# Softmax scaling: one operation for each head of a pair over all four pairs, in place of one operation for each pair of heads

## The chip, the cores and the metric

The kernel runs on one core of one Trainium2 chip. The metric is the device time of one execution in microseconds (us), of which less is better. Besides the time there is a profile of one execution: every instruction of each engine with its start and duration. The engines are called PE (TensorE; PEld is its weight load), DVE (VectorE), ACT (ScalarE), POOL (GpSimd) and SP (SyncE, which here only issues DMAs).

## What is computed

Two layers follow each other. The first is a dynamic convolution: each position of a sequence has, for each of 8 heads, 7 weights that a softmax makes; the output of a head at position s is the weighted sum of its 24 channels at positions s-6 to s. The second is a feed-forward layer with a squared ReLU.

```python
# x: (8, 4096, 192), weight_gen: (8, 4096, 8, 7), all float32
w = weight_gen - np.max(weight_gen, axis=-1, keepdims=True)
w = np.exp(w)
w = w / (np.sum(w, axis=-1, keepdims=True) + 1e-09)
...
out = np.einsum('bshk,bskhg->bshg', w, x_unf)     # x_unf: 7 positions back, per head of 24 channels
...
h = np.maximum(x @ w_in, 0.0)                     # 192 -> 2048
return (h * h @ w_out).astype(np.float32)         # 2048 -> 192
```

## The kernel before

The 32768 positions are cut into 64 sub-blocks of 512 and these into 33 blocks: two of one sub-block, then 31 of two. The instructions of all engines follow an order written out by hand: for each block a string of steps ("plan", L666 to L674, run by the loop at L782), in which a letter stands for a stage.

- L, E, S: the softmax of a part of a sequence. `load` (L213) fetches the raw weights. E is `exp` (L238) on ACT, float32, written as `ex` with the order row, pair g, tap k, head of the pair e. S is `soft` (L747): `total` (L256, a DVE reduction over the taps), `recip` (L263, a DVE reciprocal into `rcp`) and `scale` (L266, the changed function). A partition holds R consecutive positions (32 for most parts, 16 or 8 for the first ones) and 6 more of the next partition, so that 38, 22 or 14 rows are scaled. They come in pieces (`CUTS`, L682), for R = 32 of 8, 10, 10 and 10 rows, one piece per block of the main loop (`TIMES`, L685, and the default at L709).
- `scale` multiplies `ex` by the broadcast `rcp` and writes float16 into `v`, a tile [row, pair g, slot of 8, head e] (`v_big`, or `v_first` for parts of 8 rows per partition). The row stride is 64 elements, but tap k of a row lands one row further on and the slot moves with the row, which is what the strides H*SL and H*SL + 2 in the output's pattern do. Since the slots wrap every 8 rows, `scale` cuts its rows at multiples of 8 (L270): a piece of 8 rows is one cut, rows 18 to 28 are 6 and 4.
- The result goes to DRAM (`store`, L284, on SP's queue) and back as `wr` (`wr_load`, L349, SP), or, for the parts of 8 rows, straight from SBUF to SBUF (`wr_load_sbuf`, L354, DMAs at L363 on SP and POOL).
- B: `st_band` (L371, L381) multiplies `wr` by a mask on DVE into `bd`, the banded matrix of the convolution.
- C: `st_conv` (L466) or, from block 8 on, `st_conv_spread` (L429): PE multiplies `xt` by `bd` (L487, L450), then ACT and DVE copy the sum to `y` (L503, L460).
- u: `st_unit` (L508): PE makes 128 hidden features of a block, or 256 in the two small ones (L518), ACT applies the ReLU (`t`, L532, from 3 buffers that hold two units each), DVE squares (`g`, L536), two units at once up to unit 13 of a block from block 4 on.
- M: half of a quarter of the second product (`st_mm2`, L548, PE at L560) for the block before; it reads 8 of the 16 `g` of its block as weights. After the second half ACT and DVE sum and SP stores (L574, L576, L581).

DVE, ACT and POOL each execute in the order of the program. On DVE a piece of softmax thus stands between the copies, squares and bands of its block.

Of the kernel before, what the change touches and what calls it, by code (L numbers as in the profile page):

```python
# [9 lines left out]
def kernel(  # L10
# [31 lines left out]
    H, KK = weight_gen.shape[2], weight_gen.shape[3]  # L42
# [7 lines left out]
    HP = H // 2  # L50

    P = 128
# [9 lines left out]
    SL = 8  # L62
# [139 lines left out]
    class Softmax:  # L202
# [63 lines left out]
        def scale(self, lo, hi, eng):  # L266

            v = self.v
            while lo < hi:
                n = min(SL - lo % SL, hi - lo)  # L270
                for g in range(HP):
                    eng.tensor_tensor(  # L272
                        out=bass.AP(
                            tensor=v.tensor,
                            offset=v.offset + lo * H * SL + lo % SL * 2 + g * SL * 2,
                            ap=[list(v.ap[0]), [H * SL + 2, n], [H * SL, KK], [1, 2]],
                        ),
                        in0=self.ex[:, lo : lo + n, g],
                        in1=self.rcp[:, lo : lo + n, g].unsqueeze(2).broadcast_to((P, n, KK, 2)),
                        op=AluOp.mult,  # L280
                    )
                lo += n
# [312 lines left out]
    with nc.allow_low_precision("fp16 matmul pipeline"), tc.manual_schedule():  # L595
# [3 lines left out]
        for b in range(B):  # L599
            t0 = 0  # L600
            for r in PARTS.get(b, (R,)):
                v = v_first[len(parts) % 2] if r == FIRST else v_big
# [97 lines left out]
        for n, s in enumerate(parts):  # L700
            k = n - min(m for m, p in enumerate(parts) if p.b == s.b)
# [4 lines left out]
        for n, s in enumerate(parts[4:], 4):  # L706
            b, f = s.b, s.fb
            k = n - min(m for m, p in enumerate(parts) if p.b == b)
# [73 lines left out]
        for j in range(NBLK):  # L782
# [3 lines left out]
            for step in plans[j].split():  # L786
                kind, n = step[0], int(step[1:] or 0)
# [73 lines left out]
```

The softmax here doesn't subtract the row's maximum and nothing guards it: scores larger than these inputs give would overflow.

## Time and profile before

| | |
|---|---|
| time, median of 3 runs | 734.74 us (734.73 to 734.76) |
| profiled execution: its own time | 734.93 us |
| profiled execution: span from first to last instruction | 733.2 us |
| PE busy | 726.3 us, 99% of the span |
| DVE busy | 627.3 us, 86%, 856 instructions |
| ACT busy | 613.8 us, 84% |
| the changed operation, L272 on DVE | 228 instructions, in 38 groups of 4 or 8 |
| granted PE clock | 1.0 throughout |

How to read it: the busy time of an engine says how much of the span it was executing something. PE's share overstates its load, since the ends of matmuls are modelled. A timeline line gives the start in us, the duration, the engine, the line of the kernel, the operation with its output and input tile, how many such instructions are merged into the line, and in brackets how long the engine had been idle before it and what ended that. Times in groups are sums over the whole run.

### The profile page before, as it was taken

The page shows a single profiled execution, that of the slowest core. Times are in us where ns is not written, and L with a number is a line of the kernel's source. Part 1 is how long each engine was busy: PE and PEld are TensorE (multiplying, and loading weights), DVE is VectorE, ACT ScalarE, POOL GpSimd, SP SyncE. Part 2 cuts the span into 40 slices and gives each one's busy share as a digit, 9 for nine tenths or more (in the row PEclk, how much of TensorE's full clock was granted, in tenths as well). Part 3 has the DMA queues.
Part 4 walks back from the last instruction along what each step waited for, and adds up shares of the span by engine and source line. Part 5 has one row for each costly group of instructions (what it writes and reads, how often), then busy time and mean ns, then how long its engine had stood idle before and what let it go on. Part 6 is the DMA issues. An engine that isn't in the chain of part 4 may idle for free.

```text
span 733.2 us, 31124 instructions
## 1 busy us (share of the span) xinstructions
PE 726.3 (99%) x14106; PEld 528.5 (72%) x14106; DVE 627.3 (86%) x856; ACT 613.8 (84%) x724; POOL 100.5 (14%) x148
## 2 busy tenths in 40 slices
PE   8999999999999999999999999999999999999998
PEld 4767777777777777777777777777777777777777
DVE  5999898998898988888988888988889988778753
ACT  5998888988888888888888888888888888888883
POOL 7322222320001100011000010010100110001000
PEclk9999999999999999999999999999999999999999
DMA  7745444794445442455433464334544315444012
GB/s 216 124 88 132 81 63 106 143 164 119 93 73 117 105 86 64 71 131 112 69 70 72 115 125 82 62 68 122 104 87 85 59 49 120 66 87 78 30 45 67
DMA packets 126544, 68.71 MB, mean 94 GB/s; under 512 B 85193, under 2 KB 122636, under 8 KB 125900
## 3 DMA queue, kind: packets, MB, share of 16 engines
q1 hardware_dynamic: 80908, 48.12, 23.0%
q0 software_dynamic: 45360, 18.50, 21.6%
q8 instruction: 110, 1.80, 1.0%
q14 instruction: 22, 0.18, 0.1%
q10 hardware_dynamic: 144, 0.10, 0.0%
HBM read 50.18 MB, written 28.70 MB: 108 GB/s over the span
## 4 chain that ended last, share of the span: by engine, by line
PE 96%; DVE 1%; DMA 1%; ACT 1%; issue 0%; DVEq 0%
PE o L560 47%; PE h L518 45%; PE yp L450 4%; PE yp L487 1%; DVE bd L381 1%; DMA wr<-v_first 1%; ACT t L532 0%; DMA wg<-in_weight_gen_dram 0%; ACT ex L250 0%; DVE v_first L272 0%; ACT y L503 0%; DVE ssum L257 0%; DVE rcp L264 0%; DVE g L536 0%; DVE xt L347 0%
## 5 line engine op out<-in xcount | busy, mean ns | idle before, releaser
L532 ACT ACTIVATE t<-h 128x1024 f16<-128x1024 f32 x512 | 496.5, 1026 | 59.9 <-PE h L518 59.5
L560 PEld LDWEIGHTS <-g 64*128 64x128 f16 (+1 forms) x8032 | 342.5, 94 | 55.9 <-issue 2.5
L560 PE MATMUL o<-w_o,g 64*128 64x192 f16 (+1 forms) x8032 | 379.0, 243 | 0.0
L536 DVE TENSOR_TENSOR g<-t 128x2048 f16<-128x2048 f16 (+1 forms) x309 | 309.3, 1037 | 28.1 <-ACT t L532 27.9
L518 PE MATMUL h<-y,w_p 64*128 64x512 f16 x2400 | 291.7, 376 | 0.0
L518 PEld LDWEIGHTS <-w_p 64*128 64x128 f16 x2400 | 113.8, 94 | 94.9
L381 DVE TENSOR_TENSOR bd<-wr,mask 128x4160 f16<-128x4160 f16 (+3 forms) x89 | 149.4, 1703 | 4.1 <-DMA wr<-v_first 4.1
L576 DVE TENSOR_TENSOR o_sb<-o,o_sb 128x384 f32<-128x384 f32 x123 | 68.4, 556 | 60.8 <-ACT o_sb L574 59.8
L333 POOL DMA_DIRECT2D xt<-in_x_dram x62 | 52.1, 843 | 421.6 <-PE yp L450 362.5
L574 ACT COPY o_sb<-o 128x384 f32<-128x384 f32 x129 | 61.6, 478 | 46.7 <-PE o L560 45.9
L518 PE MATMUL h<-y,w_i 64*128 64x512 f16 (+1 forms) x768 | 82.1, 350 | 1.8 <-ACT t L532 0.8
L518 PEld LDWEIGHTS <-w_i 64*128 64x128 f16 x768 | 36.1, 94 | 28.6 <-issue 4.0
L450 PEld LDWEIGHTS <-xt 128*32 128x32 f16 x2000 | 24.5, 95 | 10.6 <-issue 10.6
L272 DVE TENSOR_TENSOR v_big<-ex,rcp 128x112 f16<-128x112 f32 (+5 forms) x180 | 29.8, 236 | 1.8 <-DMA vd<-v_big 0.8
L460 DVE CAST y<-yp 128x1024 f16<-128x1024 f32 x25 | 30.4, 1218 | 0.0
L450 PE MATMUL yp<-bd,xt 128*32 128x104 f16 (+1 forms) x2000 | 28.3, 210 | 0.0
L250 ACT ACTIVATE ex<-wg 128x560 f32<-128x560 f32 (+4 forms) x38 | 25.9, 682 | 1.7 <-DMA wg<-in_weight_gen_dram 1.7
L257 DVE TENSOR_REDUCE ssum<-ex 128x80 f32<-128x560 f32 (+4 forms) x38 | 25.3, 666 | 2.2 <-ACT ex L250 2.2
L460 ACT CAST y<-yp 128x1024 f16<-128x1024 f32 x25 | 25.2, 1006 | 0.0
L264 DVE RECIPROCAL rcp<-ssum 128x80 f32<-128x80 f32 (+4 forms) x38 | 22.8, 600 | 1.3
L323 POOL DMA_DIRECT2D xt<-in_x_dram x7 | 3.9, 553 | 124.7 <-PE yp L450 109.7
L363 POOL DMA_DIRECT2D wr<-v_first x31 | 16.9, 563 | 16.0 <-DVE v_first L272 15.8
(34 smaller groups left out, 97.3 us busy)
## 6 DMA issues: line engine op xcount, KB each, us to landing
out_dram<-o_sb SPq DMA_DIRECT2D x63, 384.0 KB
xt<-in_x_dram POOLq DMA_DIRECT2D x42, 240.0 KB, 5.0
wg<-in_weight_gen_dram SPq DMA_DIRECT2D x4, 1064.0 KB
xt<-in_x_dram POOLq DMA_DIRECT2D x20, 192.0 KB, 4.7
wr<-vd SPq DMA_DIRECT2D x38, 80.0 KB
vd<-v_big SPq DMA_DIRECT2D x5, 512.0 KB
y<-y SPq DMA_DIRECT2D x100, 24.0 KB
wg<-in_weight_gen_dram SPq DMA_DIRECT2D x5, 392.0 KB
```

What stands on the lines that cost most here:

```text
L250: nc.scalar.activation(out=self.ex[:, lo:hi].rearrange("p r g k e -> p (r g) k e"), in_=self.wg[:, lo:hi].rearrange("p r (g e) k -> p (r g ...
L272: eng.tensor_tensor(out=bass.AP(tensor=v.tensor, offset=v.offset + lo * H * SL + lo % SL * 2 + g * SL * 2, ap=[list(v.ap[0]), [H * SL + 2, ...
L333: eng.dma_start(out=dst[:, first:last], in_=ap)
L381: nc.vector.tensor_tensor(out=bd_t[j][:, H * lo : H * (lo + len(tiles) * n)].rearrange("p (g m c) -> p g m c", g=shape[1], c=2 * SL), in0= ...
L450: nc.tensor.matmul(out=yp[p0 : p0 + 32, k - k0, a:b], lhsT=x_t[s][:, i, c0 : c0 + 32], rhs=bd[:, head // 2, e, 0 : b - a], start=True, sto ...
L460: copy(out=y[:, k0 : k0 + 2], in_=yp)
L518: nc.tensor.matmul(out=h[:, half, jj * th : (jj + 1) * th], lhsT=w_in_chunk(w, u * per + jj, slot, half), rhs=y_t[j][r0 : r0 + RT, k, 0:th ...
L532: nc.scalar.activation(out=t1[:, e], in_=h, func=ActF.Relu)
L536: nc.vector.tensor_tensor(out=g[:, a : e + 1], in0=t1[:, a : e + 1], in1=t1[:, a : e + 1], op=AluOp.mult)
L560: nc.tensor.matmul(out=oo[:, cc * Dm : (cc + 1) * Dm], lhsT=g[r0 : r0 + n, cc * P : (cc + 1) * P], rhs=w_o[r0 : r0 + n, fc, :], start=(fc ...
L574: nc.scalar.copy(out=o_sb, in_=o[0][:, c])
L576: nc.vector.tensor_tensor(out=o_sb, in0=o[1][:, c], in1=o_sb, op=AluOp.add)
```

## The change

In `scale` the loop over the four pairs of heads becomes a loop over the two heads of a pair. Nothing else differs but the line numbers after it, which are 3 higher.

```diff
                 n = min(SL - lo % SL, hi - lo)
-                for g in range(HP):
+                for e in (0, 1):
                     eng.tensor_tensor(
                         out=bass.AP(
                             tensor=v.tensor,
-                            offset=v.offset + lo * H * SL + lo % SL * 2 + g * SL * 2,
-                            ap=[list(v.ap[0]), [H * SL + 2, n], [H * SL, KK], [1, 2]],
+                            offset=v.offset + lo * H * SL + lo % SL * 2 + e,
+                            ap=[list(v.ap[0]), [H * SL + 2, n], [SL * 2, HP], [H * SL, KK]],
                         ),
-                        in0=self.ex[:, lo : lo + n, g],
-                        in1=self.rcp[:, lo : lo + n, g].unsqueeze(2).broadcast_to((P, n, KK, 2)),
+                        in0=self.ex[:, lo : lo + n, :, :, e].rearrange("p r g k -> p (r g) k"),
+                        in1=self.rcp[:, lo : lo + n, :, e]
+                        .rearrange("p r g -> p (r g)")
+                        .unsqueeze(2)
+                        .broadcast_to((P, n * HP, KK)),
                         op=AluOp.mult,
                     )
```

A cut of n rows took four operations of 14n elements per partition and takes two of 28n. Before, the innermost loop ran over the two heads of a pair: two neighbours in `ex` (float32), two neighbours in `rcp`, two neighbours in `v` (float16, 4 bytes together), then a hop of 128 bytes in `v` to the next tap. After, the innermost loop runs over the seven taps of one head: every second element of `ex` (8 bytes apart), the same element of `rcp` seven times, and in `v` single elements of 2 bytes that lie 128 bytes apart.

## The prediction

> **What bounds the kernel now.** I read the page first (busy times, chain of waits), then the groups by form, then two stretches of the timeline: the start and one block of the steady part.
>
> ```profile
> PE 726.3 (99%) x14106; PEld 528.5 (72%) x14106; DVE 627.3 (86%) x856; ACT 613.8 (84%) x724; POOL 100.5 (14%) x148
> ...
> PE 96%; DVE 1%; DMA 1%; ACT 1%; issue 0%; DVEq 0%
> PE o L560 47%; PE h L518 45%; PE yp L450 4%; PE yp L487 1%; DVE bd L381 1%; DMA wr<-v_first 1%; ACT t L532 0%; DMA wg<-in_weight_gen_dram 0%; ACT ex L250 0%; DVE v_first L272 0%; ACT y L503 0%; DVE ssum L257 0%; DVE rcp L264 0%; DVE g L536 0%; DVE xt L347 0%
> ```
>
> The chain that ended last is PE for 96%. DVE is on it for 1%, and the changed line only at the start. So a shorter scaling can win next to nothing; a longer one costs only where DVE becomes so late that PE waits. The groups by form give the price of the operation now, by its width:
>
> ```profile
> L272 DVE TENSOR_TENSOR v_big<-ex,rcp 128x112 f16<-128x112 f32 x60 | 12.5, 271 | 1.4 <-DMA vd<-v_big 0.8
> L272 DVE TENSOR_TENSOR v_big<-ex,rcp 128x84 f16<-128x84 f32 x52 | 9.3, 241 | 0.2
> L272 DVE TENSOR_TENSOR v_big<-ex,rcp 128x56 f16<-128x56 f32 x32 | 4.8, 211 | 0.1
> L272 DVE TENSOR_TENSOR v_big<-ex,rcp 128x28 f16<-128x28 f32 x20 | 2.4, 181 | 0.0
> ```
>
> From 28 to 112 elements it grows by 90 ns, 1.07 ns an element over 151 ns fixed. The timeline shows four of 112 in 0.83 us, so they start (0.83 - 0.271) / 3 = 0.186 us apart: 85 ns of each overlap the next, and a group takes 85 ns + 66 ns for each operation + 1.07 ns for each element.
>
> The timeline of a steady block (start, duration, engine, line):
>
> ```profile
> 406.42 1.22 DVE L272 TENSOR_TENSOR v_big<-ex,rcp 128x84 f16<-128x84 f32 x8
> ...
> 407.56 2.35 DVE L536 TENSOR_TENSOR g<-t 128x2048 f16<-128x2048 f16 x2
> ...
> 409.83 0.55 DVE L576 TENSOR_TENSOR o_sb<-o,o_sb 128x384 f32<-128x384 f32 x1
> ...
> 410.93 2.52 DVE L536 TENSOR_TENSOR g<-t 128x2048 f16<-128x2048 f16 x3 [0.55 <-ACT t L532]
> ...
> 412.71 1.47 PEld L560 LDWEIGHTS <-g 64*128 64x128 f16 x32
> 412.93 1.48 PE L560 MATMUL o<-w_o,g 64*128 64x192 f16 x32
> ```
>
> After the scaling DVE stands idle once, for 0.55 us, then squares the last three units of the block until 413.45. PE's next M starts at 412.93; its last eighth, which needs the last square, starts 7/8 of some 1.31 us later, at 414.08. So that M has 0.63 us in hand; less 0.22 us by which the weight load goes ahead and some 0.06 us of signalling, 0.35 us. DVE may come 0.55 + 0.35 = 0.9 us late from this scaling before PE waits. The other steady blocks repeat this (0.38 us idle after the few groups of 1.28 us).
>
> **What the Trainium skill says.** (1) "Vector Engine (DVE) Microarchitecture Reference", 5.2 Measured stream behaviour: two-source operations take 1.0417 ns a column plus about 75 ns an instruction after overlap. The trace agrees: 1.07 and 66. (2) The same section, on the SBUF access granule: a port streams at full rate only if consecutive elements come in runs of at least two adjacent 4-byte words; a destination that hops at every element takes 1.71 ns a column (4 KiB hops) or 2.50 (hops of 24 words), all three ports hopping 1.98. The trace has no such write; today's, two halves of one word and then a hop, runs at full rate. (3) "SBUF — State Buffer", Door 1, on 16-byte cachelines: full rate needs two hits on a line. The trace's L257, which reads every second float32 of `ex`, agrees: 448 elements in 610 ns and 560 in 726, 1.04 ns each.
>
> **The change, part by part.**
>
> Removed and added: 228 operations become 114 of twice the width. Over all widths they carry 60x112 + 24x112 + (52+24)x84 + 32x56 + 20x28 + 8x70 + 8x42 = 19,040 elements, the same as before. Fewer instructions save 114 x 66 ns = 7.5 us of DVE. Against that stands s, the time per element. Full rate, 1.07 ns, is the low end: then DVE saves 7.5 us. The write now hops 128 bytes at every element, the first source steps by two words, the second repeats a word. Page prices: 1.71 to 2.50 for such a destination alone; if the sources add to it as in the page's three-port row (1.98 / 1.71 = 1.16), up to 2.9. I take 2.3, an estimate inside these prices, as 32 words lie nearer to the row with 24 than to the one with 4 KiB. Then DVE gets 19,040 x 1.23 = 23.4 us more and 7.5 less: +16 us. It breaks even at s = 1.07 + 7.5/19.04 = 1.46.
>
> Steady groups (560 elements, 8 operations now, 4 then): 85 + 4x66 + 560 s. At 1.07: 0.95 us (before: 1.22); at 2.3: 1.64, +0.42; at 2.9: 1.97, +0.75. All are below the 0.9 us in hand: hidden by DVE's idle time and M's reserve. Without this cover it would cost 0.42 us in each of some 17 blocks, 7 us. The price that uses up the cover is (1.22 + 0.9 - 0.349) / 0.56 = 3.2 ns an element. The reserve of the `t` buffers at unit 14 is larger (1.8 us or more in these blocks).
>
> Behind the scaling on SP's queue stand the store to DRAM and the `wr` loads; bands need those half a block (some 11 us) later, so +0.4 us is hidden. POOL's DMAs of `wr` are issued when the scaling ends and move with it; none is added.
>
> The start (784 elements, 8 operations to 4) is on the chain:
>
> ```profile
> 6.70 1.46 DVE L272 TENSOR_TENSOR v_first<-ex,rcp 128x112 f16<-128x112 f32 x8
> ...
> 8.19 1.93 SPq L363 DMA_DIRECT2D wr<-v_first  x3
> ...
> 11.98 1.47 ACT L650 CAST w_i<-w_st 128x1536 f16<-128x1536 f32 x1 [0.15 <-DMA w_st<-in_moe_w_in_dram]
> 12.27 2.60 DVE L381 TENSOR_TENSOR bd<-wr,mask 128x832 f16<-128x832 f16 x5 [4.11 <-DMA wr<-v_first]
> ```
>
> It becomes 0.35 + 0.784 s: 1.19 us at 1.07 (-0.27), 2.15 at 2.3 (+0.69), 2.62 at 2.9 (+1.16). But the first `wr` lands 4.1 us after its issue, where the median of these DMAs is 2.6: it stands in SP's DMA queue behind the weights `w_st`, whose last landing ends a wait at 11.98. So up to some 1.4 us later issue is hidden, and an earlier one gains little. I take 0.
>
> Early blocks with less cover. (a) The second part (22.88 to 24.34) delays the bands that end at 33.17; PE's convolution starts at 33.87. Reserve 0.7; +0.69 just fits: some 0.1. (b) Around 98 to 104 DVE is full: two groups of 448 elements (86.11 and 101.68, each +0.42 at 2.3) with 0.2 us idle between them, ahead of an M with 0.78 - 0.28 = 0.5 us in hand: 0.84 - 0.2 - 0.5 = 0.1. (c) The other early groups of 448 have 0.5 us or more of idle or reserve ahead: 0. Sum +0.2 us. At 2.5 it is some 0.5, at 2.9 some 1.3 (0.5 at each of (a) and (b), 0.3 elsewhere).
>
> The sum against the profiled execution: 734.93 + 0.2 = 735.1; that stands 0.19 above the median, so 734.74 + 0.2 = 734.9.
>
> **The rivals.**
>
> (A) Forecast: hopping writes at 1.7 to 2.9 ns, hidden. 734.7 to 736.0, likeliest 734.9. For it: PE's 96% and DVE's idle time; against it: how close the reserves are to what is added.
>
> (B) Full rate: short 4-byte hops are free as L257's reads are, or the write port merges them. DVE saves 7.5 us of busy time, PE doesn't care; the start gains 0.27 us at most, half of it behind `w_st`: 734.6. Speaks for it that today's writes hop every 2 elements without cost.
>
> (C) Slower: 2-byte writes that share no word cost over 3.2 ns, for instance because a partial word has to be read first (nothing here shows that). It happens at M after each block's last square: at 4 ns a group takes 2.59 us, +1.37, of which 0.47 passes 0.9 us and stops PE, in some 17 blocks 8 us, with the early ones 10: 745. At 3.3 it is 737. It decides from 3.2 ns. Against it: the largest page price is 2.5.
>
> (D) Faster by over 0.2%: DVE is full from 18 to 43 us and relief there would have to reach PE. The groups there save 0.27 + 0.13 + 0.1 us: too little.
>
> That the change doesn't do what it says: built, it has 114 operations of 128 x (n x 4 x 7) in the same places; excluded.
>
> **How the numbers follow.** 0.2%, 1.5 us, is about what a measurement of this kernel can tell from no change. A 0.60, of which 0.06 above 1.5 us; B 0.14; C 0.22, of which 0.20 above; D 0.04. So faster 0.04, same 0.70, slower 0.26. The likeliest time is 734.9. Leaving out D and the part of C beyond 3.4 ns (about 0.15) gives 734.3 to 738.0.
>
> **What would show it.** L272 has 114 instructions; one of 224 elements takes 151 + 224 s: 0.39 us at full rate, 0.67 at 2.3, 0.87 at the limit of 3.2. DVE busy rises by some 16 us. The idle time before the third-last square of a block shrinks from 0.55 to some 0.1, and the wait list shows no PE wait for `g`. The first bands still start near 12.3. I am wrong if an instruction of 224 takes over 0.87 us, if the first bands move with the scaling, or if the M after a block's end starts late, block after block.

## The result and the profile after

The changed kernel takes 767.23 us (median of 6 runs, 765.56 to 767.91) against 734.74: 1.0442 times, with a 95% interval of 1.0429 to 1.0456, so 32.5 us more. The prediction said 734.9, with a range up to 738.0. The profiled execution took 765.56 us with a span of 763.9, 30.7 more than the span before.

The page of the changed kernel, its busy times and its chain:

```profile
PE 733.5 (96%) x14106; PEld 567.0 (74%) x14106; DVE 671.3 (88%) x742; ACT 614.1 (80%) x724; POOL 99.9 (13%) x148
...
PE 67%; DVE 24%; DMA 3%; issue 3%; ACT 2%; POOL 1%; DVEq 0%; POOLq 0%; SPq 0%
PE o L563 36%; PE h L521 28%; DVE g L539 6%; DVE v_big L272 6%; PE yp L453 3%; DVE o_sb L579 3%; DVE v_first L272 3%; DVE rcp L264 2%; DVE ssum L257 2%; DMA wr<-v_first 2%; DVE bd L384 1%; ACT o_sb L577 1%; DMA vd<-v_big 1%; POOL wr L366 1%; ACT t L535 0%
```

DVE executes 114 instructions fewer and is busy 44 us longer. It was on the chain for 1% and now is for 24%. Its groups by form say why (last columns: busy time, mean ns of one):

```profile
L272 DVE TENSOR_TENSOR v_big<-ex,rcp 128x224 f16<-128x224 f32 x30 | 32.7, 1283 | 4.2 <-DMA vd<-v_big 3.6
L272 DVE TENSOR_TENSOR v_big<-ex,rcp 128x168 f16<-128x168 f32 x26 | 23.1, 1083 | 0.2
...
L272 DVE TENSOR_TENSOR v_big<-ex,rcp 128x112 f16<-128x112 f32 x16 | 10.3, 838 | 0.1
...
L272 DVE TENSOR_TENSOR v_big<-ex,rcp 128x56 f16<-128x56 f32 x10 | 4.4, 638 | 0.0
```

From 56 to 224 elements the operation grows by 645 ns: 3.84 ns an element, where it was 1.07. An operation of 112 elements, a form that both kernels have, took 271 ns and takes 838. Now the wait lists. PE's longest wait of the changed kernel is not in the list of the kernel before at all (us in total, times, longest):

```profile
PE o L563 <- DVE o_sb L579: 19.6, 24, 3.6
```

The timeline of the changed kernel shows why, in the block just before the one that the prediction showed (both scale 10 rows, and before the change both run alike):

```profile
407.24 2.68 DVE L272 TENSOR_TENSOR v_big<-ex,rcp 128x224 f16<-128x224 f32 x4
...
409.54 2.55 DVE L539 TENSOR_TENSOR g<-t 128x2048 f16<-128x2048 f16 x2
...
411.78 0.24 PE L563 MATMUL o<-w_o,g 64*128 64x192 f16 x1
412.01 0.55 DVE L579 TENSOR_TENSOR o_sb<-o,o_sb 128x384 f32<-128x384 f32 x1
412.48 2.41 DVE L539 TENSOR_TENSOR g<-t 128x2048 f16<-128x2048 f16 x3
412.61 1.48 PE L563 MATMUL o<-w_o,g 64*128 64x192 f16 x31 [0.59 <-DVE o_sb L579]
```

PE starts an M at 411.78 and comes through one matmul. The product is summed in two banks of PSUM, the memory that PE writes to: ACT copies the first (L577), DVE adds the second (L579), and the next M may write the second bank only when this add has read it. The add stands on DVE behind the scaling and two squares. It ends at 412.56, and 0.05 us later PE goes on. The same scaling, add and M before:

```profile
384.33 1.22 DVE L272 TENSOR_TENSOR v_big<-ex,rcp 128x112 f16<-128x112 f32 x8
...
387.74 0.55 DVE L576 TENSOR_TENSOR o_sb<-o,o_sb 128x384 f32<-128x384 f32 x1
...
388.87 1.48 PE L560 MATMUL o<-w_o,g 64*128 64x192 f16 x32
```

The add ended at 388.29, so it had 0.58 us in hand. From the start of the scaling to the end of the add it was 3.96 us and is 5.32, 1.36 more; the block (from one scaling to the next, 384.33 to 406.42 before, 407.24 to 430.16 now) takes 22.92 us instead of 22.09, 0.83 more. 1.36 - 0.83 = 0.53: what was in hand, but for the signalling.

The trace can be read block by block, if the start of the second matmul of each M is compared in the two traces. (A block counts here with the M of its own units, which runs in the block after it.) The delay is 4.2 us by the end of block 1, 9.3 by the end of block 4, 13.1 after block 5 (which adds 3.8), 16.8 after block 8, and 30.7 after block 27, the last with a scaling. In the steady part, from block 12 on, each block with a piece of 10 rows adds 0.83, each with a piece of 8 rows only 0.1: there the shorter sum, reciprocal and scaling leave the add some 0.6 us more. Blocks 9 to 11, whose pieces are cut otherwise, add 0.9 to 1.3 each.

### The profile page after: what moved, and what is told of

Its sections match the earlier page's. It is cut to its first block, busy times and chain, and to the rows that moved or that the text cites. A ratio compares the mean times of both kernels' runs of the same rounds, so it can differ in the third digit from the quotient of the medians.

```text
span 763.9 us, 31010 instructions
## 1 busy us (share of the span) xinstructions
PE 733.5 (96%) x14106; PEld 567.0 (74%) x14106; DVE 671.3 (88%) x742; ACT 614.1 (80%) x724; POOL 99.9 (13%) x148
## 4 chain that ended last, share of the span: by engine, by line
PE 67%; DVE 24%; DMA 3%; issue 3%; ACT 2%; POOL 1%; DVEq 0%; POOLq 0%; SPq 0%
PE o L563 36%; PE h L521 28%; DVE g L539 6%; DVE v_big L272 6%; PE yp L453 3%; DVE o_sb L579 3%; DVE v_first L272 3%; DVE rcp L264 2%; DVE ssum L257 2%; DMA wr<-v_first 2%; DVE bd L384 1%; ACT o_sb L577 1%; DMA vd<-v_big 1%; POOL wr L366 1%; ACT t L535 0%
## 5 line engine op out<-in xcount | busy, mean ns | idle before, releaser
L563 PE MATMUL o<-w_o,g 64*128 64x192 f16 (+1 forms) x8032 | 391.9, 243 | 20.5 <-DVE o_sb L579 19.6
L563 PEld LDWEIGHTS <-g 64*128 64x128 f16 (+1 forms) x8032 | 354.2, 94 | 71.5 <-issue 31.8
L539 DVE TENSOR_TENSOR g<-t 128x2048 f16<-128x2048 f16 (+1 forms) x309 | 314.0, 1060 | 13.3 <-ACT t L535 13.2
L521 PE MATMUL h<-y,w_p 64*128 64x512 f16 x2400 | 298.0, 376 | 0.0
L521 PEld LDWEIGHTS <-w_p 64*128 64x128 f16 x2400 | 141.4, 94 | 73.5
L579 DVE TENSOR_TENSOR o_sb<-o,o_sb 128x384 f32<-128x384 f32 x123 | 69.2, 563 | 60.8 <-ACT o_sb L577 60.2
L577 ACT COPY o_sb<-o 128x384 f32<-128x384 f32 x129 | 61.6, 478 | 44.4 <-PE o L563 42.2
L521 PE MATMUL h<-y,w_i 64*128 64x512 f16 (+1 forms) x768 | 83.8, 350 | 2.5 <-ACT t L535 1.3
L272 DVE TENSOR_TENSOR v_big<-ex,rcp 128x224 f16<-128x224 f32 (+5 forms) x90 | 69.1, 1035 | 4.6 <-DMA vd<-v_big 3.6
L521 PEld LDWEIGHTS <-w_i 64*128 64x128 f16 x768 | 42.7, 94 | 24.6 <-issue 5.5
L272 DVE TENSOR_TENSOR v_first<-ex,rcp 128x224 f16<-128x224 f32 (+1 forms) x24 | 22.9, 1179 | 0.3
```

The costliest lines, as they stand in the source:

```text
L272: eng.tensor_tensor(out=bass.AP(tensor=v.tensor, offset=v.offset + lo * H * SL + lo % SL * 2 + e, ap=[list(v.ap[0]), [H * SL + 2, n], [SL ...
L521: nc.tensor.matmul(out=h[:, half, jj * th : (jj + 1) * th], lhsT=w_in_chunk(w, u * per + jj, slot, half), rhs=y_t[j][r0 : r0 + RT, k, 0:th ...
L539: nc.vector.tensor_tensor(out=g[:, a : e + 1], in0=t1[:, a : e + 1], in1=t1[:, a : e + 1], op=AluOp.mult)
L563: nc.tensor.matmul(out=oo[:, cc * Dm : (cc + 1) * Dm], lhsT=g[r0 : r0 + n, cc * P : (cc + 1) * P], rhs=w_o[r0 : r0 + n, fc, :], start=(fc ...
L577: nc.scalar.copy(out=o_sb, in_=o[0][:, c])
L579: nc.vector.tensor_tensor(out=o_sb, in0=o[1][:, c], in1=o_sb, op=AluOp.add)
```

## The experiments

**What makes the operation dear.** Six kernels change L272 alone. The first two split writes from reads. In the first, with the writes of the changed kernel, the edit is

```diff
-                        in0=self.ex[:, lo : lo + n, :, :, e].rearrange("p r g k -> p (r g) k"),
-                        in1=self.rcp[:, lo : lo + n, :, e]...
+                        in0=self.ex[:, lo : lo + n, 2 * e : 2 * e + 2].rearrange("p r g k c -> p r (g k c)"),
+                        in1=self.ex[:, lo : lo + n, 2 - 2 * e : 4 - 2 * e].rearrange("p r g k c -> p r (g k c)"),
```

> Writes as in the changed kernel (single float16 elements 128 bytes apart), both sources read in order instead (two different quarters of the exponentials, so the weights are wrong). Theory W, the write alone makes the price: an operation of 224 elements stays at 1.29 us and the time near 766 us. Rival S, the strided and repeated sources make it: 0.39 us and the time near 735 us. Both together: in between, some 0.7 us.

The second keeps the sources and writes to neighbours:

```diff
-                            offset=v.offset + lo * H * SL + lo % SL * 2 + e,
-                            ap=[list(v.ap[0]), [H * SL + 2, n], [SL * 2, HP], [H * SL, KK]],
+                            offset=v.offset + lo * H * SL + e * H * SL // 2,
+                            ap=[list(v.ap[0]), [H * SL, n], [KK, HP], [1, KK]],
```

> Sources as in the changed kernel (every second exponential, the reciprocal seven times), written to neighbouring float16 elements (so the weights lie in wrong places). Theory W: an operation of 224 elements takes some 0.39 us, since the sources run at full rate, and the time goes back to 734 to 735 us. Rival S: 1.29 us and near 766 us.

The groups by form, first with the write alone changed as in the changed kernel, then with the reads alone:

```profile
L272 DVE TENSOR_TENSOR v_big<-ex 128x224 f16<-128x224 f32 x30 | 31.7, 1248 | 3.6 <-DMA vd<-v_big 3.6
```

```profile
L272 DVE TENSOR_TENSOR v_big<-ex,rcp 128x224 f16<-128x224 f32 x30 | 10.4, 388 | 1.3 <-DMA vd<-v_big 0.7
```

1248 of the 1283 ns come with the write; with the changed reads and a dense write the rate is still 1.07 ns an element. The times, one execution each: 760.8 us and 734.2, beside 734.1 for the kernel before. Theory W holds, though the first time is 5 us under the 766 expected: in its trace a steady block loses 0.65 us, not 0.83. The second kernel also shows what a cheaper scaling is worth: DVE is busy 620.9 us, 6.4 less than before, and the time is the same within 0.2 us.

The other four change the write further: whole words of float32 at the same 128 bytes (by a comparison in place of the product), and half words (single float16 elements, half of a 4-byte word) at 4, 8 and 16 bytes. The edits in short, each to the output's pattern:

```diff
+ whole words:  v32 = v viewed as float32; [H * SL // 2 + 1, n], [SL, HP], [H * SL // 2, KK]; op=AluOp.is_ge
+ 4 bytes:      offset + e; [H * SL, n], [KK * 2, HP], [2, KK]
+ 8 bytes:      offset + e; [2 * H * SL, n], [4 * KK, HP], [4, KK]
+ 16 bytes:     offset + e; [H * SL, n], [2, HP], [8, KK]
```

> As the changed kernel, but each write is a whole float32 word, 128 bytes from the last (the operation is a comparison, whose result is 0 or 1, instead of the product; both heads write the same words, so the weights are wrong). If the hop of 128 bytes makes the price: 1.29 us for 224 elements. If it is the half word: at most the 1.7 to 2.5 ns that the skill gives for hopping words, so 0.5 to 0.75 us.

> As the changed kernel, but the float16 elements are written 4 bytes apart instead of 128 (so the weights lie in wrong places): still half a word each, but four on a line of 16 bytes. If the half word makes the price: 1.29 us for 224 elements. If it is the hop to another line: near 0.39 us.

> As the changed kernel, but the float16 elements are written 16 bytes apart (so the weights lie in wrong places): every element on another line of 16 bytes. If a half word on another line is what costs: 1.29 us for 224 elements and some 766 us. If it takes a long hop: near 0.41 us and 735 us.

> As the changed kernel, but the float16 elements are written 8 bytes apart (so the weights lie in wrong places): two elements on a line of 16 bytes. If two on a line are enough, as the skill says of lines: near 0.41 us for 224 elements. If the unit is 8 bytes: 1.29 us.

The groups of the four, in the order words, 4, 16 and 8 bytes:

```profile
L273 DVE TENSOR_TENSOR v_big<-ex,rcp 128x224 f32<-128x224 f32 x30 | 17.2, 572 | 3.3 <-DMA vd<-v_big 2.2
```

```profile
L272 DVE TENSOR_TENSOR v_big<-ex,rcp 128x224 f16<-128x224 f32 x30 | 10.7, 409 | 1.4 <-DMA vd<-v_big 0.8
```

```profile
L272 DVE TENSOR_TENSOR v_big<-ex,rcp 128x224 f16<-128x224 f32 x30 | 32.4, 1268 | 4.0 <-DMA vd<-v_big 3.4
```

```profile
L272 DVE TENSOR_TENSOR v_big<-ex,rcp 128x224 f16<-128x224 f32 x30 | 17.5, 683 | 2.2 <-DMA vd<-v_big 1.7
```

With the operations of 56 elements from the same lists (264, 218, 639 and 307 ns) the slopes are:

| write, one element after the other | ns an element | 128x224, ns | time of the kernel, us |
|---|---|---|---|
| float16 neighbours (reads as changed) | 1.07 | 388 | 734.2 |
| float16, 4 bytes apart | 1.14 | 409 | 735.0 |
| float32 word, 128 bytes apart | 1.83 | 572 | 736.0 |
| float16, 8 bytes apart | 2.24 | 683 | 735.2 |
| float16, 16 bytes apart | 3.74 | 1268 | 767.4 |
| float16, 128 bytes apart (the change) | 3.84 | 1283 | 767.2 |

The last row is a median of six executions, the others are one each; the kernel before took 734.1 us beside the 4-byte, dense and whole-word cases, and 735.0 (median of nine) beside those of 8 and 16 bytes. Neither the half word alone (4 bytes apart: 1.14) nor the hop alone (a whole word: 1.83) makes this price. Half words that each lie on another 16 bytes make it, and 128 bytes cost hardly more than 16. Why that is so, no run shows. The 8 byte case came out between the two answers expected: two elements on a line of 16 bytes are not enough for the full rate of such writes, otherwise than the prediction's third point has it for lines. Each kernel up to 2.24 ns stays within 2 us of the kernel before: the loss starts somewhere between 2.24 and 3.74.

**Is it DVE's lateness that PE pays for, or something else in the scattered writes?** The kernel before, with each scaling operation done twice:

```diff
-                for g in range(HP):
+                for g in (*range(HP), *range(HP)):
```

> The kernel before with every scaling operation done twice, so DVE is kept as late by cheap writes: a group of 560 elements takes 85 + 16 x 66 + 1120 x 1.07 ns = 2.34 us, 1.12 more than before (the changed kernel: 1.47 more). Theory Q, a late DVE delays the add that frees the PSUM bank of the second product, with 0.63 us in hand for 560 elements and 1.24 for 448: each 560 block loses some 0.5 us, the early part 4 to 6, together 745 to 750 us. Rival I, the scattered writes disturb the other engines at SBUF: 735 us.

It took 753.46 us, 1.0246 times the kernel before (1.0230 to 1.0263): rival I falls for the steady part, for these writes are the old ones. A steady block lost 0.60 with a group 1.13 us longer, so again 0.53 us was in hand, and blocks with 8 rows lost nothing. The total is 3 us above the range expected; the early blocks lost 10.7, not 4 to 6. Its wait list has the same entry:

```profile
PE o L560 <- DVE o_sb L576: 11.4, 22, 2.7
```

**Which wait.** The changed kernel, with the add taken off the PSUM bank, its place and length kept:

```diff
-            nc.vector.tensor_tensor(out=o_sb, in0=o[1][:, c], in1=o_sb, op=AluOp.add)
+            nc.vector.tensor_tensor(out=o_sb, in0=o_sb, in1=o_sb, op=AluOp.add)
```

> The changed kernel, but the DVE add of the output reads the SBUF tile twice and not the PSUM bank (so the second half of the sum is left out); it keeps its place and length on DVE. Theory Q: PE no longer waits for this add; a steady block of 560 elements loses what the next wait, for the last square of a block, leaves uncovered: 1.47 - 0.9 = 0.57 us or less instead of 0.83, and much of the loss between blocks 2 and 8 goes: 748 to 758 us. Rival T, DVE's total work is the bound: 766 us, nothing changes.

It took 751.66 us, 1.0223 times (1.0203 to 1.0244), with DVE busy 671.0 us as in the changed kernel. Steady blocks lose 0.07 us instead of 0.83. So there the add makes all but 0.07 us of the loss. The next wait, the one that the prediction named, has more in hand than the 0.9 us reckoned: DVE is as late as before, 1.36 us. PE's wait for the add is gone; one for the squares is left, in the early blocks:

```profile
PE o L563 <- DVE g L539: 6.1, 8, 2.1
```

There the gain is small: 13.6 us of delay after block 8 instead of 16.8. Blocks 2 and 3 lose 0.1 us together instead of 3.0, but blocks 0, 1, 4, 5 and 6 lose 12.2 instead of 11.3. What those lose is not this wait alone: without it PE is held up by others.

**Is the loss local?** Two kernels apply the change to some parts only, and one keeps all its work but moves some of it.

```diff
+                if self.r == R:          # the other kernel: if self.r > FIRST:
+                    for e in (0, 1):     # one operation per head
...
+                else:
+                    for g in range(HP):  # one operation per pair
```

> One operation per head only in the parts with 32 rows per partition (the sequences 3 to 7), one per pair in the early parts. The delays of the second product in the changed kernel's trace grow by 16.8 us up to block 8 and by 13.9 from block 9 to 27. Theory Q, the losses are local and add up: 734.7 + 13.9 = 748.6 us. If the late losses come from lateness carried over from the early blocks: 740 us or less.

> One operation per pair in the parts of 8 rows per partition, which feed blocks 0 to 5, and one per head in all later parts (16 and 32 rows). In the changed kernel's trace the delays of the second product reach 9.3 us by the end of block 4. Theory Q, losses are local and add up: 767.2 - 9 = 758 us, and the early loss is that of these parts' lateness. If the later blocks would lose the time anyway, because DVE is already full there: 762 us or more.

```diff
-                for e in (0, 1):
+                for e in heads:
...
+            if s.r == R and 0 < lo and hi < s.rh:
+                s.scale(lo, hi, nc.vector, (0,))       # second head: a step at the start of the next block
+                s.rest = [*getattr(s, "rest", ()), (lo, hi)]
+                return
```

> The changed kernel with the same operations, but in the middle pieces of the parts with 32 rows the second head is scaled at the start of the next block, where DVE stands idle for 1.5 us ahead of an add. DVE's work is the same. Theory Q: the ten blocks so treated lose nothing, the last piece of each part still does: 767.2 - 8 = 759 us. Rival T, DVE's total work is the bound: 767 us.

They took 748.42 us (1.0174, 1.0159 to 1.0190), 758.02 us (1.0309, 1.0291 to 1.0326) and 759.14 us (1.0316, 1.0298 to 1.0333), each within 0.2 us of what theory Q gave. That is closer than they can be measured: the executions of the second lie between 756.7 and 761.0 us. By the differences the parts of 8 rows cost some 9 us, those of 16 rows 9 to 10 (758.0 - 748.4), those of 32 rows 14. The first and the last agree with what the changed kernel's trace shows for their blocks (9.3 and 13.9). The third has the changed kernel's operations, DVE busy 672.8 us, and is 8 us faster than it; its treated blocks lose 0.02 us or less. So what PE pays for there is not the work on DVE, but what stands ahead of the add when M needs it.

**One knock-on.** Block 5 adds 3.8 us. One piece of 38 is put back to one operation per pair:

```diff
+                if self.b == 1 and self.r == R // 2 and lo == 2 * SL:
+                    for g in range(HP):  # one operation per pair
```

> The changed kernel, but one piece of the 38, the last of the second sequence's 16-row part, is scaled per pair as before. In the changed kernel's trace its store to DRAM lands 7.2 us after its issue (before: 5.3), behind weight loads that POOL issues at the same moment, and DVE waits 3.6 us for it, then PE 3.6. Theory K, that is a knock-on of this one piece being late: block 5 loses some 1 us instead of 3.8 and the time is 764 to 765 us. Rival: the piece costs only its own 0.8 us: 766.5 us or more.

It took 764.01 us (1.0384, 1.0369 to 1.0398), 3.2 less than the changed kernel, and in its trace block 5 adds 1.7 us; in the other traces with this piece scaled per head and half words far apart it adds 3.4 to 6.3, but for the one without the add (2.1). The two timelines, first of the changed kernel:

```profile
134.90 0.34 SPq L289 DMA_DIRECT2D vd<-v_big  x1
...
142.07 2.16 DVE L272 TENSOR_TENSOR v_big<-ex,rcp 128x224 f16<-128x224 f32 x2 [3.60 <-DMA vd<-v_big]
```

```profile
135.21 0.34 SPq L302 DMA_DIRECT2D vd<-v_big  x1
...
141.19 2.18 DVE L285 TENSOR_TENSOR v_big<-ex,rcp 128x224 f16<-128x224 f32 x2 [1.60 <-DMA vd<-v_big]
```

The store reads `v_big`, of which there is one, so the next part's scaling waits for it. In the changed kernel it was issued 0.76 us after the first of POOL's weight loads, in the other 0.19 us before it. It landed 7.2 us after its issue instead of 6.0, and DVE waited 3.6 us instead of 1.6, then PE. That fits theory K; that the store shares the DMA engines with these loads is read from the times, not tried.

## Why the prediction was wrong, point by point

- **PE is the bound, a cheaper scaling wins nothing: right.** The kernel with the scaling at full rate took 734.2 us beside 734.1. At the start, too, the reasoning nearly held: the first scaling takes 2.24 us more (6.73 to 10.43), but the first bands start at 12.55 instead of 12.27, for their `wr` lands 2.1 us after its issue instead of 4.1.
- **The time per element, "I take 2.3": this failed first.** It measured 3.84. The prices of the Trainium skill's "Vector Engine (DVE) Microarchitecture Reference", 5.2, are for words of 4 bytes, and the whole-word run lies among them (1.83 for a hop of 128 bytes, where the page has 1.71 for one of 4 KiB and 2.50 for one of 24 words). Applying them to half words was the mistake. Rival C named half of the cause that was left out, writes that share no word, and gave it 0.22; the runs show that such writes cost 1.14 ns when they lie 4 bytes apart, and 3.7 to 3.8 only from 16 bytes on. That the old writes hop too and cost nothing was read as reassurance. They are whole words of two elements, so one word goes out every 2.14 ns, and a hopping word was measured to take 1.83; that fits.
- **"DVE may come 0.9 us late": this failed as well.** The nearer wait was overlooked: the add L576, in the same timeline that the prediction shows, at 409.83; it ends 0.58 us ahead of PE's M at 410.96. The search was for who reads the squares, not for what PE needs free before it can write. At 0.53 us, the limit for s is near 2.5 ns, not 3.2. This is one reason why rival C, worked out at 4 ns, gave only 745: it has 0.47 us a block where 0.83 was measured. The other is the early blocks.
- **The early blocks, "+0.2 us": 16.8 us.** They were costed at 2.3 ns; at 3.84 each reserve named there is passed, DVE stays full from block to block, and one store falls behind other loads. Rival C's 2 us for them was far off too. For the blocks up to 8 what each microsecond waited for is only shown in part. Taking the add away won some 3 us, moving the store at block 5 some 3. PE's waits up to 175 us name the add for 7.8 us (3.6 of them behind that store) and squares, bands and `xt` for 3.1. The rest stays open.
- **At its own price the forecast holds.** The write at 8 bytes costs 2.24 ns an element, and that kernel took 735.2 us (one execution), beside 735.0 for the kernel before (median of nine); 734.9 was forecast over 734.74. It says nothing for the wait that was named, since at 2.24 ns neither reserve is used up.
- The count of instructions (114) and the order on the engines went as said. The fixed cost and the overlap did not: by the widths of 56 and 224 an operation has 423 ns beside its elements, where it had 151. Four operations of 2 x 168 and 2 x 112 elements take 3.84 us singly and 2.69 together, so some 0.38 us of each lies under the next, where it was 0.085. The two nearly cancel: some 40 ns are left for each operation, where the prediction has 66.

## What to carry to other kernels

An elementwise operation is priced by its output pattern as much as by its length: fewer, wider instructions can lose, as here, if they turn whole words into half words that jump. Before an engine with idle time is given more work, follow each of its operations in that stretch to whoever waits for it, the ones that only free a buffer included; the smallest reserve among them, not the idle share, says how much fits. A price taken from a table belongs to the element size that the table was measured with.

## What the runs showed of the hardware that was not expected

On DVE, float16 elements written one by one cost 1.14 ns each at 4 bytes, 2.24 at 8, 3.74 at 16 and 3.84 at 128 bytes; a float32 word at 128 bytes costs 1.83. The reads of the same operation, every second float32 and a value repeated seven times, ran at 1.07 with a dense write; for these reads the rule of two adjacent words, in the prediction's second point, does not hold. After writes 128 bytes apart the following operation is slower too: two squares took 2.55 us right behind the scaling and 2.35 elsewhere.
